# Fused attention and two MLPs on one core: the shared tile of a head pair is moved to second place, and the next pair's Q and K transposes and first scores are moved behind other work

## The chip, the cores and the metric

The kernel runs on one core of a Trainium2 chip. A core has TensorE (PE; its weight loads, which overlap the matmuls, are listed as PEld), VectorE (DVE), ScalarE (ACT), GpSimd (POOL) and SyncE (SP, which here only issues DMAs). The metric is the time of one execution on the device in microseconds (us), as the median of several runs.

## The reference, cut to what matters

```python
B, H, S, D = 4, 8, 576, 64                       # q, k, v: [B, H, S, D]; f: [B, H, S]
scores = (1 / np.sqrt(D)) * np.matmul(q, k.transpose(0, 1, 3, 2))
cum = np.cumsum(np.log(np.clip(f, 0.0001, 1.0)), axis=-1)
decay = cum[:, :, :, None] - cum[:, :, None, :]
scores = np.where(causal, -1e9, scores + decay)  # causal: keys behind the query
attn = softmax(scores)                           # max, exp, sum + 1e-9
x = (attn @ v) laid out as [B * S, H * D]        # 2304 tokens x 512
h = x @ w_in;  x = (h - tanh(h)) @ w_out         # first MLP, 512 -> 2048 -> 512
h = x @ w2_in; out = relu(h) ** 2 @ w2_out       # second MLP, same sizes
```

All of it is float32. The kernel splits operands into a high and a low part of a shorter float format and adds three products, so many matmuls come in twos and threes.

## The kernel before, in words

**Work units.** Attention is cut into 64 units: for each of 32 heads, first the queries 0 to 255 (`hf` 0), then the queries 256 to 575 (`hf` 1, L462). The change concerns the second half, units 32 to 63. Two heads that follow each other make a pair: the even head and the odd head. A unit of the second half has tiles of 128 queries: tile 2 (384 keys), tile 3 (512 keys), and the last 64 queries of *both* heads of a pair share tile 4 (576 keys), which is worked with the even head. Each tile is a **slot** (L465). The slots of a pair are, in order, tiles 2, 3 and 4 of the even head and tiles 2 and 3 of the odd head, named e2, e3, e4, o2 and o3 in this document. A ring of five buffers `Pb` (L369) holds the slots' scores; the one with 640 columns must be that of tile 4 (L466).

**What happens to a slot.** `decay` (L532) writes the decay and the causal mask into the ring's buffer on GpSimd, two slots ahead. It reads a row of `cum` that `load_neg` (L516) has spread over 128 partitions by DMA; there are two such buffers, and the end of `decay` (L559 to L565) loads the row of a later unit. `s_atom` (L732) makes the scores on TensorE from K1 (high part), KLh (low part) and X (Q, both parts); `softmax_of` (L653) takes the maximum on VectorE (L673), the exponential on ScalarE (L682), one over the sum on VectorE and the product with it on GpSimd (L698). Two slots later `pt_atom` (L750) transposes the tile on TensorE (L779); ScalarE copies the high part into PT[0] (L788) and VectorE the low part into PT[1] (L789). For tile 4 a further 128 x 128 block (L774) goes to PT[2] (L793, L795). When the last slot of a head has been transposed, `pv_atoms` (L851) multiplies with the values: atom 0 uses PT[0] in four matmuls (L862) and then PT[2] in one (L866), atom 1 uses PT[1] in four (L862).

**What happens once a pair.** `qk_atoms` (L607) transposes raw k (L629, four matmuls) and raw q (L640, three) of the next pair. ScalarE and VectorE then write K1, KLh and X (L619, L621), and two DMAs copy K1's halves between partitions (L644, L645). There is one K1 and one KLh, so this comes behind the last scores of the pair before.

**What sets the order.** `attn_stream` (L899) yields atoms with a cost (about the columns that TensorE takes). `mlp1_stream` yields atoms of the first MLP (lines L1011 and L1051), 1536 units each in the blocks that lie beside the second half. The loop at L1484 runs the next attention atom when the MLP units done have reached its due time: past the units 0 to 31, 4.65 times the cost of one MLP block (64 x 1536 = 98304 units) is spread evenly over the cost of the 16 pairs. A pair costs 18048 units: scores 5888 (768, 1024 and 2304 for tiles 2, 3 and 4; then 768, 1024), k and q transposes 1792 (1024, 768), values 5504 (even head 1472 and 1216, odd head 1536 and 1280), transposes 4864 (768 for tile 2, 1024 for tile 3, 1280 for tile 4). What follows an atom on other engines is put behind it by a number of steps (`LAG`, L58). From this program order a scheduler makes each engine's list before the run: it goes by priority, and an instruction that it holds not to be ready lets later ones pass. Tiles of PSUM with tag "a" (scores, transposes, values) share four banks.

In the slot loop of `attn_stream` (L908), slot i does in this order: `decay` of slot i + 2; the scores of slot i; at a pair's last slot the k and q transposes of the next pair; the values of a head that has become ready; at an even head's last slot `split_v`, which writes the head pair's values VH; the transposes of slot i - 2.

Of the kernel before, what the change touches and what calls it, by code (L numbers as in the profile page):

```python
# [10 lines left out]
F32 = mybir.dt.float32  # L11
# [7 lines left out]
B, H, S, D = 4, 8, 576, 64  # L19
NT, DM, DFF = B * S, H * D, 2048  # L20
P = 128
# [12 lines left out]
TILES = ([(0, 128, 0, 128), (1, 128, 128, 256)],  # L34
         [(2, 128, 0, 384), (3, 128, 0, 512), (4, 128, 0, 576)])
# [4 lines left out]

PTC = {2: (448, 3), 3: (192, 4)}
XB = (64, 768)
RING = 5
ENDS = (0.5, 1.0, 1.8, 6.45)
UP = (2, 0.1, 1.0)
HOT = 200
# [64 lines left out]
def fused_kernel(ctx: ExitStack, tc: tile.TileContext, q, k, v, f, w1i, w1o, w2i, w2o, out):  # L111
# [8 lines left out]
    ap = actx.enter_context(tc.tile_pool(name="ap", bufs=1))  # L120
# [245 lines left out]
    ident = ap.tile([P, P], F32, name="ident")  # L366
    ccol = ap.tile([P, 5, B * H], F32, name="ccol")
    lfT = ap.tile([P, 5, B * H], F32, name="lfT")
    Pb = [ap.tile([P, 640 if i == RING - 1 else 512], F32, name=f"Pb{i}") for i in range(RING)]  # L369
    mask4 = ap.tile([P, D], F32, name="mask4")  # L370

    st0 = [ap.tile([P, 2, 4], F32, name=f"sp{i}") for i in range(4)]
# [3 lines left out]
    PT, X = [], []  # L376
# [4 lines left out]
    negs = {}  # L381
# [80 lines left out]
    units = [(b, hf, h) for hf in range(2) for b in range(B) for h in range(H)]  # L462
    NU = len(units)
    NH0 = B * H
    slots = [(n, ts) for n in range(NU) for ts in ([TILES[0]] if n < NH0 else [[t] for t in TILES[1][: 3 - n % 2]])]  # L465
    assert all(i % RING == RING - 1 for i, (n, ts) in enumerate(slots) if ts[0][0] == 4)  # L466
    slot0 = {}
    for i, (n, _) in enumerate(slots):
        slot0.setdefault(n, i)
# [42 lines left out]
    def load_done(n):  # L512

        return n >= NH0 or n % 4 == 2

    def load_neg(n):  # L516
        b, hf, h = units[n]
        row = b * H + h
        if hf == 0:
            if n % 2 == 0:  # L520
                t = ap.tile([P, S], F32, tag="neg", name=f"neg_{n}", bufs=2)
                src = cscr[row : row + 1, :256]
                load(t[:, :512].rearrange("p (h k) -> p h k", h=2),
                     bass.AP(tensor=src.tensor, offset=src.offset, ap=[[0, P], [S, 2], [1, 256]]))
                for i in range(2):
                    negs[n + i] = t[:, 256 * i : 256 * i + 256]
        else:
            t = ap.tile([P, S], F32, tag="neg", name=f"neg_{n}", bufs=2)
            nc.sync.dma_start(t, cscr[row : row + 1, :].to_broadcast([P, S]))
            negs[n] = t  # L530

    def decay(i):  # L532
        n, ts = slots[i]
        b, hf, h = units[n]
        if n not in negs:
            load_neg(n)
        t = negs[n]
        pb = Pb[i % RING]
        if len(ts) > 1:
            for ti, rows, o, w in ts:  # L540
                nc.gpsimd.tensor_scalar(pb[:, o : o + w], t[:, :w], ccol[:, ti, b * H + h : b * H + h + 1], 1.0,
                                        op0=ALU.add, op1=ALU.mult)
            x = pb[:, 0:P]
            dg = bass.AP(tensor=x.tensor, offset=x.offset, ap=[x.ap[0], [2 * P, 2], [1, P]])
            nc.gpsimd.affine_select(dg, dg, pattern=[[0, 2], [-1, P]], compare_op=ALU.is_ge, fill=MASK,
                                    base=0, channel_multiplier=1)
        elif ts[0][0] < 4:
            ti, rows, o, w = ts[0]
            nc.gpsimd.tensor_scalar(pb[:rows, o : o + w], t[:rows, :w], ccol[:rows, ti, b * H + h : b * H + h + 1], 1.0,
                                    op0=ALU.add, op1=ALU.mult)  # L550
            dg = pb[:rows, o + ti * P : o + ti * P + rows]
            nc.gpsimd.affine_select(dg, dg, pattern=[[-1, rows]], compare_op=ALU.is_ge, fill=MASK,
                                    base=0, channel_multiplier=1)
        else:
            for x, m in ((slice(0, D), n + 1), (slice(D, P), n)):
                c = b * H + h + m - n
                nc.gpsimd.tensor_scalar(pb[x, :S], negs[m][x, :], ccol[x, 4, c : c + 1], 1.0, op0=ALU.add, op1=ALU.mult)
            nc.gpsimd.tensor_tensor(pb[:, 512:S], in0=pb[:, 512:S], in1=mask4, op=ALU.add)
        nxt = n + 1  # L559
        if n >= NH0:  # L560
            nxt = n + 1 if n % 2 == 0 and ts[0][0] == 2 else n + 2 if ts[0][0] == 4 else NU
        elif slots[i + 1][0] == n:
            nxt = NU
        if nxt < NU and nxt not in negs:
            load_neg(nxt)  # L565

    def split_v(n):
        b, hf, h = units[n]
# [84 lines left out]
    def softmax_of(i):  # L653

        n = slots[i][0]
        b, hf, h = units[n]
        pb = Pb[i % RING]
        hh = h % 2
# [91 lines left out]
    def pt_atom(i):  # L750

        n, ts = slots[i]
        pb = Pb[i % RING]

# [96 lines left out]
    def pv_atoms(n):  # L851
        b, hf, h = units[n]
        hh = h % 2
        nq = NQ[1]
        box = {}

        def a(hl):
            if hl == 0:
                box["t"] = bank("a", 4, f"pv_{n}")
            t = box["t"]  # L860
            for c, (c0, ql, w) in PVC[hh].items():
                nc.tensor.matmul(t[:, ql : ql + w], lhsT=VH[:, hh, c].rearrange("p a d -> p (a d)"),  # L862
                                 rhs=PT[hl][:, c0 : c0 + w], start=hl == 0 and c == 0, stop=hl == 1 and c == 3)
            if hl == 0:
                ql = 256 - 256 * hh
                nc.tensor.matmul(t[:, ql : ql + D], lhsT=VH[:, hh, 4].rearrange("p a d -> p (a d)"),  # L866
                                 rhs=PT[2][:, D - D * hh : 2 * D - D * hh], start=False, stop=False)
            if hl == 1:
                cw.later(LAG['pv'], ev)

        def ev():
            t = box["t"]
            if hh == 0:
                xs_box["t"] = ap.tile([P, 320], F32, tag="xs", name=f"xs_{n}", bufs=2)
            xs = xs_box["t"]
            own = slice(hh * D, hh * D + D)
            oth = slice(D - hh * D, 2 * D - hh * D)
            tmp = ap.tile([P, 320], F32, tag="xtmp", name=f"xt_{n}", bufs=1)
            nc.scalar.activation(tmp[own, :nq], t[oth, :nq], AF.Copy)  # L879

            def fin():
                for c0, d0, w in ((0, 0, nq),) if hh == 0 else ((D, 0, 256), (0, 256, D)):
                    nc.vector.tensor_tensor(xs[own, d0 : d0 + w], t[own, c0 : c0 + w], tmp[own, c0 : c0 + w], op=ALU.add)
                if hh == 1:
                    pair_done(b, hf, h // 2, xs)
            cw.later(LAG['pvadd'], fin)

        cost = sum(max(256, w) for _, _, w in PVC[hh].values())
        return [(cost + 256, lambda: a(0)), (cost, lambda: a(1))]

    def pair_done(b, hf, p, xs):
        if (b, hf) == (0, 0):
# [6 lines left out]
    def attn_stream():  # L899

        yield 0, first_sums, 0
        yield 0, (lambda: (decay(0), decay(1), feed.upload(UP[0]))), 0
        for c, a in kq_atom(0):
            yield c, a, 0

        NS = len(slots)
        pvs, ready = 0, []
        for i in range(NS + 3):  # L908
            if i < NS:
                n, ts = slots[i]  # L910
                last = i + 1 == NS or slots[i + 1][0] != n
                if i == SUMS:
                    yield 0, more_sums, pvs
                if i + 2 < NS:
                    yield 0, (lambda i=i: decay(i + 2)), pvs
                if n % 2 == 0 and n + 2 < NH0:
                    for c, a in kq_atom(n + 2):
                        yield c, a, pvs
                    if load_done(n + 2):
                        yield 0, (lambda: cw.later(LAG['load'], lambda: load_next("qk"))), pvs  # L920
                if n >= NH0:
                    yield *s_atom(i), pvs
                elif n % 2 == 0:
                    yield *s_pair(i), pvs
                if last and n % 2 == 1 and NH0 <= n + 1 < NU:
                    for c, a in qk_atoms(n + 1):
                        yield c, a, pvs
                    yield 0, (lambda: load_next("qk")), pvs
            for m in ready:
                if m >= NH0:  # L930
                    for c, a in pv_atoms(m):
                        yield c, a, pvs
                    pvs += 1
                elif m % 2 == 1:
                    for c, a in pair_atom(m - 1):
                        yield c, a, pvs
                    pvs += 2
            ready = []
            if i < NS and last and n % 2 == 0 and n >= NH0:
                yield 0, (lambda n=n: split_v(n)), pvs  # L940
            if 2 <= i < NS + 2:
                yield *pt_atom(i - 2), pvs
                m = slots[i - 2][0]
                if i - 1 == NS or slots[i - 1][0] != m:
                    ready.append(m)


    xhl = {}
# [585 lines left out]
```

## Time and profile before

| what | us |
|---|---|
| median of three runs | 1048.13 |
| the runs | 1045.79, 1048.13, 1048.20 |
| the profiled execution, its own time | 1042.0 |
| its span, first to last instruction | 1040.3 |
| VectorE busy in the span | 739.5 |
| ScalarE busy | 576.2 |
| GpSimd busy | 425.3 |

The span lies 1.7 us below the time of the execution that was profiled, and that execution lies 3.8 us below the fastest of the three runs. Times in views count from the span's start. In a timeline row the columns are start, duration, engine, line, operation, output and inputs, shape and count; what stands in square brackets is the engine's idle time just before and who ended it. A matmul's end is modelled, so rows of matmuls overlap. A DMA's row on SPq is its issue.

### The profile page before, as it was taken

The numbers are of one execution on the slowest core, as the hardware profiler recorded it, in microseconds if no ns is written. First come the engines' busy times: TensorE is split into PE (matmuls) and PEld (weight loads), VectorE is DVE, ScalarE is ACT, GpSimd is POOL, SyncE is SP. The second block draws the span as 40 slices with busy tenths as digits, with TensorE's granted clock in tenths as the row PEclk, the third lists the DMA queues.
The fourth block names the chain that finished last, engine by engine and source line by source line (L and its number), as shares of the span: only waits on it lengthen the run. The fifth ranks groups of instructions, "written<-read, shape, count | busy, mean of one in ns | idle before, by whom it ended". The sixth has DMA issues, their size and how long they took to land.

```text
span 1040.3 us, 20254 instructions
## 1 busy us (share of the span) xinstructions
PE 1000.9 (96%) x7134; PEld 952.9 (92%) x7134; DVE 739.5 (71%) x1533; ACT 576.2 (55%) x1185; POOL 425.3 (41%) x587
## 2 busy tenths in 40 slices
PE   7989999999999999999999999999999888999998
PEld 5778899999999999999999887999999888999998
DVE  4896963676677766766757578668667969978773
ACT  5885954565666665666645456536455545333331
POOL 3664532354545454555423133395965630000000
PEclk9998999999999999999999999999999989999999
DMA  8946743243343343333203332556777875444431
GB/s 232 275 127 213 213 140 86 72 118 83 78 125 91 90 115 83 107 91 90 78 14 87 102 122 81 169 174 242 226 260 280 274 243 177 142 127 149 132 102 41
DMA packets 184949, 146.97 MB, mean 141 GB/s; under 512 B 86320, under 2 KB 159344, under 8 KB 184848
## 3 DMA queue, kind: packets, MB, share of 16 engines
q1 hardware_dynamic: 184800, 145.65, 46.5%
q8 instruction: 56, 0.92, 0.4%
q14 instruction: 45, 0.37, 0.1%
q10 hardware_dynamic: 48, 0.03, 0.0%
HBM read 101.00 MB, written 39.92 MB: 135 GB/s over the span
## 4 chain that ended last, share of the span: by engine, by line
PE 63%; DVE 8%; POOL 8%; DMA 7%; ACT 6%; issue 6%; SPq 2%; POOLq 0%; ACTq 0%; DVEq 0%
PE o L1371 16%; PE h L1011 14%; PE y L1051 14%; PE pv L862 3%; POOL g L1271 3%; PE r L1221 2%; PE pt L779 2%; PE s L744 2%; PE pv L824 2%; PE s L713 2%; PE s L745 2%; DMA gscr<-g 2%; DMA wscr<-wfull 1%; SPq L151 1%; ACT K L619 1%
## 5 line engine op out<-in xcount | busy, mean ns | idle before, releaser
L1051 PE MATMUL y<-ghl,w 128*128 128x256 f32 (+1 forms) x1536 | 243.1, 302 | 2.8 <-DVE ghl L1032 2.2
L1051 PEld LDWEIGHTS y<-ghl,w 128*128 128x128 f32 x1536 | 210.4, 191 | 16.1 <-DVE ghl L1032 3.5
L1011 PE MATMUL h<-x,w 128*128 128x256 f32 x1344 | 194.9, 289 | 5.5 <-POOL w L228 4.9
L1011 PEld LDWEIGHTS h<-x,w 128*128 128x128 f32 x1344 | 173.5, 191 | 10.5 <-POOL w L228 6.4
L1371 PE MATMUL o<-ws,gc 128*128 128x256 f32 x864 | 117.1, 284 | 0.0
L1347 ACT ACTIVATE gc<-graw 128x1792 fp32r<-128x1792 f32 x35 | 59.4, 1703 | 101.9 <-PE o L1371 59.7
L1221 PE MATMUL r<-yt,ws 128*128 128x384 f32 x576 | 109.1, 337 | 1.6 <-DVE g L1232 1.5
L1371 PEld LDWEIGHTS o<-ws,gc 128*128 128x128 f32 x864 | 110.1, 193 | 0.0
L1271 POOL TENSOR_TENSOR g<-g 128x384 f32<-128x384 f32 (+1 forms) x72 | 84.0, 1185 | 52.6 <-ACT g L1235 47.3
L1221 PEld LDWEIGHTS r<-yt,ws 128*128 128x128 f32 x576 | 101.4, 189 | 2.4 <-DVE g L1232 2.3
L1371 PE MATMUL o<-wq,gc 128*128 128x256 f32 x648 | 92.5, 285 | 5.9 <-ACT gc L1347 5.1
L682 ACT ACTIVATE Pb<-Pb,st 128x384 f32<-128x384 f32 (+2 forms) x80 | 55.2, 690 | 71.1 <-DVE st L673 71.0
L698 POOL TENSOR_SCALAR Pb<-Pb,st 128x384 f32<-128x384 f32 (+2 forms) x80 | 55.2, 690 | 92.0 <-ACT xt L879 45.7
L1371 PEld LDWEIGHTS o<-wq,gc 128*128 128x128 f32 x648 | 84.4, 193 | 6.8 <-ACT gc L1347 5.5
L1221 PE MATMUL r<-yt,wq 128*128 128x384 f32 x432 | 85.0, 341 | 5.1 <-DVE g L1232 3.7
L1221 PEld LDWEIGHTS r<-yt,wq 128*128 128x128 f32 x432 | 77.3, 192 | 6.1 <-DVE g L1232 4.0
L673 DVE CUSTOM_DVE_ANT_0 Pb<-s,Pb 128x128 f32<-128x128 f32 (+4 forms) x144 | 66.8, 479 | 20.2 <-PE s L745 15.0
L1348 DVE TENSOR_TENSOR gc<-graw,gc 128x1792 fp32r<-128x1792 f32 x35 | 71.0, 2032 | 12.9 <-ACT gc L1347 12.8
L1024 DVE TENSOR_TENSOR g<-h,g 128x512 f32<-128x512 f32 x72 | 49.5, 688 | 32.1 <-ACT g L1021 31.5
L1235 ACT ACTIVATE g<-g 128x384 f32<-128x384 f32 x72 | 36.4, 522 | 62.7 <-DVE g L1232 62.4
L1021 ACT ACTIVATE g<-h 128x512 f32<-128x512 f32 x72 | 42.7, 593 | 35.8 <-PE h L1011 30.1
L1032 DVE TENSOR_TENSOR ghl<-g,ghl 128x512 fp32r<-128x512 f32 x72 | 53.7, 746 | 10.6 <-ACT ghl L1028 10.3
(167 smaller groups left out, 1903.5 us busy)
## 6 DMA issues: line engine op xcount, KB each, us to landing
graw<-gscr SPq DMA_DIRECT2D x144, 128.0 KB, 2.4
wraw<-in_moe_w_in_dram SPq DMA_DIRECT2D x32, 512.0 KB, 4.6
wraw<-in_moe_w_out_dram SPq DMA_DIRECT2D x32, 512.0 KB, 5.9
neg<-cscr SPq DMA_DIRECT2D x32, 288.0 KB, 3.3
gscr<-g SPq DMA_DIRECT2D x48, 192.0 KB, 4.0
gscr<-g SPq DMA_DIRECT2D x24, 384.0 KB, 3.5
qk<-in_k_dram SPq DMA_DIRECT2D x48, 128.0 KB, 2.8
v<-in_v_dram SPq DMA_DIRECT2D x48, 128.0 KB, 2.5
```

Of the source, the lines that this page charges most:

```text
L673: nc.vector.tensor_tensor_reduce(out=d, in0=t[:rows, src : src + m], in1=d, scale=-0.125, scalar=3.0e38 if j == 0 else stat(0, x)[:rows], ...
L682: nc.scalar.activation(d, d, AF.Exp, bias=stat(len(parts) - 1, x)[:rows], scale=-1.0, accum_out=stat(2, x)[:rows])
L698: nc.gpsimd.tensor_scalar(d, d, r, 1.0, op0=ALU.mult, op1=ALU.mult)
L1011: nc.tensor.matmul(o, lhsT=win(fc, wh, dc), rhs=xpart(j, dc, xh), start=dc == 0 and wh + xh == 0, stop=dc == ND - 1 and wh == 1)
L1024: nc.vector.tensor_tensor(g, t, g, op=ALU.subtract)
L1032: nc.vector.tensor_tensor(ghl[:, 1], g, ghl[:, 0].bitcast(F32), op=ALU.subtract)
L1051: nc.tensor.matmul(o, lhsT=wout(fc, wh, i * P, P), rhs=ghl[:, xh, fj * n : fj * n + n], start=s == 0 and fj == 0 and wh + xh == 0 and i % ...
L1221: nc.tensor.matmul(t, lhsT=wprod(1, p, k, wh)[:, dc * P : (dc + 1) * P], rhs=yt[i, k][:, xh, dc], start=k in FIRST and dc == 0 and wh + xh ...
L1271: nc.gpsimd.tensor_tensor(g, in0=g, in1=g, op=ALU.mult)
L1347: nc.scalar.activation(hi, t[:, 1:8], AF.Copy)
L1348: nc.vector.tensor_tensor(lo, in0=t[:, 1:8], in1=hi.bitcast(F32), op=ALU.subtract)
L1371: nc.tensor.matmul(o, lhsT=gc[n][gh][:, GWHERE[k], e], rhs=wprod(2, 2 * q + e, k, wh), start=q == 0 and e == 0 and gh + wh == 0 and c0 == ...
```

## The change

The order of a pair's slots becomes e2, e4, e3, o2, o3, and the wide buffer of the ring is the one with index 3. In the slot loop the k and q transposes of the next pair move to the end of slot o3, behind the transposes of slot e3; the scores of e2 move to the end of their slot, behind the even head's values of the pair before and the transposes of o2. PT[2]'s matmul moves from atom 0 of the values to the end of atom 1. The row of `cum` for a head is now loaded by `decay` of tile 3 of the head two places before it, and the first two rows of the second half by the last unit of the first half.

```diff
-RING = 5
+RING, WIDE = 5, 3
...
-    slots = [(n, ts) for n in range(NU) for ts in ([TILES[0]] if n < NH0 else [[t] for t in TILES[1][: 3 - n % 2]])]
-    assert all(i % RING == RING - 1 for i, (n, ts) in enumerate(slots) if ts[0][0] == 4)
+    slots = [(n, ts) for n in range(NU) for ts in ([TILES[0]] if n < NH0 else [[TILES[1][x]] for x in ((0, 2, 1), (0, 1))[n % 2]])]
+    assert all(i % RING == WIDE for i, (n, ts) in enumerate(slots) if ts[0][0] == 4)
...
-        nxt = n + 1
         if n >= NH0:
-            nxt = n + 1 if n % 2 == 0 and ts[0][0] == 2 else n + 2 if ts[0][0] == 4 else NU
-        elif slots[i + 1][0] == n:
-            nxt = NU
-        if nxt < NU and nxt not in negs:
-            load_neg(nxt)
+            nxt = (n + 2,) if ts[0][0] == 3 else ()
+        else:
+            nxt = (n + 1,) if n + 1 < NH0 else (n + 1, n + 2)
+        for m in nxt:
+            if m < NU and m not in negs:
+                load_neg(m)
...
-                                 rhs=PT[hl][:, c0 : c0 + w], start=hl == 0 and c == 0, stop=hl == 1 and c == 3)
-            if hl == 0:
+                                 rhs=PT[hl][:, c0 : c0 + w], start=hl == 0 and c == 0, stop=False)
+            if hl == 1:
                 ql = 256 - 256 * hh
                 nc.tensor.matmul(t[:, ql : ql + D], lhsT=VH[:, hh, 4].rearrange("p a d -> p (a d)"),
-                                 rhs=PT[2][:, D - D * hh : 2 * D - D * hh], start=False, stop=False)
-            if hl == 1:
+                                 rhs=PT[2][:, D - D * hh : 2 * D - D * hh], start=False, stop=True)
                 cw.later(LAG['pv'], ev)
...
-        return [(cost + 256, lambda: a(0)), (cost, lambda: a(1))]
+        return [(cost, lambda: a(0)), (cost + 256, lambda: a(1))]
...
-                if n >= NH0:
+                late = n >= NH0 and n % 2 == 0 and ts[0][0] == 2
+                if n >= NH0 and not late:
                     yield *s_atom(i), pvs
-                elif n % 2 == 0:
+                elif n < NH0 and n % 2 == 0:
                     yield *s_pair(i), pvs
-                if last and n % 2 == 1 and NH0 <= n + 1 < NU:
-                    for c, a in qk_atoms(n + 1):
-                        yield c, a, pvs
-                    yield 0, (lambda: load_next("qk")), pvs
...
+            if i < NS and late:
+                yield *s_atom(i), pvs
+            if i < NS and last and n % 2 == 1 and NH0 <= n + 1 < NU:
+                for c, a in qk_atoms(n + 1):
+                    yield c, a, pvs
+                yield 0, (lambda: load_next("qk")), pvs
```

## Rows read from the trace of the kernel before

**Rows 1.** The page's first part: each engine's busy time, share of the span, instructions.

```profile
PE 1000.9 (96%) x7134; PEld 952.9 (92%) x7134; DVE 739.5 (71%) x1533; ACT 576.2 (55%) x1185; POOL 425.3 (41%) x587
```

**Rows 2.** Stretches: start and end, sum, each engine's busy time, clock, DMA share, GB/s.

```profile
core 0: us, PE busy (x) PEld busy (x) DVE busy (x) ACT busy (x) POOL busy (x), PEclk, DMA share, GB/s
...
170.00:546.00 376.00, 370.62 (x2944) 362.50 (x2943) 255.39 (x705) 226.49 (x533) 179.59 (x304) 1.00 0.34 89
...
830.00:865.00 35.00, 27.68 (x164) 26.87 (x165) 26.70 (x36) 17.91 (x27) 10.19 (x9) 0.85 0.76 249
```

**Rows 3.** Groups of weight loads, 170 to 546 us; last column: idle before, releasers.

```profile
L862 PEld LDWEIGHTS pv<-PT,VH 128*128 128x128 f32 x256 | 38.7, 188 | 3.2 <-DVE PT L789 1.9 <-issue 0.6
...
L744 PEld LDWEIGHTS s<-K,X 128*128 128x128 f32 x128 | 24.2, 189 | 4.7 <-issue 4.2 <-ACT PT L793 0.4
...
L866 PEld LDWEIGHTS pv<-PT,VH 128*128 128x128 f32 x32 | 6.0, 187 | 2.1 <-DVE PT L795 2.1
```

**Rows 4.** Groups of matmuls, 170 to 546 us, the same columns.

```profile
L862 PE MATMUL pv<-PT,VH 128*128 128x320 f32 (+1 forms) x256 | 47.4, 309 | 1.2 <-DVE PT L789 0.9
...
L744 PE MATMUL s<-K,X 128*128 128x288 f32 (+2 forms) x128 | 42.9, 347 | 2.9 <-DMA K<-K 2.1 <-DVE X L621 0.7
...
L866 PE MATMUL pv<-PT,VH 128*128 128x64 f32 x32 | 7.0, 219 | 1.1 <-DVE PT L795 1.1
```

**Rows 5.** Timeline: q's transposes of one pair to its first scores.

```profile
355.67 0.49 PE L640 MATMUL tq<-ident,qk 128*128 128x128 f32 x3
...
356.83 0.60 PE L779 MATMUL pt<-ident,Pb 128*128 128x128 f32 x4
...
357.18 1.67 PE L1011 MATMUL h<-x,w 128*128 128x256 f32 x12
...
358.25 1.58 SPq L645 DMA_DIRECT2D K<-K  x1
...
358.69 1.84 PE L1051 MATMUL y<-ghl,w 128*128 128x256 f32 x14
...
359.03 0.59 ACT L788 ACTIVATE PT<-pt 128x512 fp32r<-128x512 f32 x1
...
359.33 1.06 DVE L621 TENSOR_TENSOR X<-tq,X 64x256 fp32r<-64x256 f32 x3
...
361.11 0.19 PEld L744 LDWEIGHTS s<-K,X 128*128 128x128 f32 x1 [0.79 <-issue]
361.14 0.41 PE L744 MATMUL s<-K,X 128*128 128x384 f32 x1 [0.61 <-DMA K<-K]
...
361.47 0.69 DVE L789 TENSOR_TENSOR PT<-pt,PT 128x512 fp32r<-128x512 f32 x1
```

**Rows 6.** Timeline: o3's transposes, e4's scores and normalisation, the odd head's values.

```profile
365.56 0.60 PE L779 MATMUL pt<-ident,Pb 128*128 128x128 f32 x4
...
365.92 0.96 PE L1011 MATMUL h<-x,w 128*128 128x256 f32 x6
...
366.67 0.58 ACT L788 ACTIVATE PT<-pt 128x512 fp32r<-128x512 f32 x1
366.71 0.29 PE L744 MATMUL s<-K,X 128*128 128x288 f32 x1
...
367.28 0.69 DVE L789 TENSOR_TENSOR PT<-pt,PT 128x512 fp32r<-128x512 f32 x1
...
369.91 0.75 PE L862 MATMUL pv<-PT,VH 128*128 128x320 f32 x4
...
370.53 0.96 PE L1051 MATMUL y<-ghl,w 128*128 128x256 f32 x6
...
370.91 0.76 POOL L698 TENSOR_SCALAR Pb<-Pb,st 128x576 f32<-128x576 f32 x1
```

**Rows 7.** Waits in SP's queue, 170 to 546 us, and landing times of L645.

```profile
SPq L529 <- POOL Pb L552: 46.3, 10, 5.4
...
SPq L644 <- ACT K L619: 9.5, 12, 1.9
...
DMA to landing us min/median/max: 2.4/2.4/3.4
```

More of the change, by code (lines that the diff above doesn't have):

```diff
@@ L368, in fused_kernel @@
     lfT = ap.tile([P, 5, B * H], F32, name="lfT")
-    Pb = [ap.tile([P, 640 if i == RING - 1 else 512], F32, name=f"Pb{i}") for i in range(RING)]
+    Pb = [ap.tile([P, 640 if i == WIDE else 512], F32, name=f"Pb{i}") for i in range(RING)]
     mask4 = ap.tile([P, D], F32, name="mask4")
```

## The prediction, made before the changed kernel was run

> Short names: e2, e3, e4 are the even head's slots of a pair, o2 and o3 the odd head's; e4 holds the tile that both heads share.
>
> **What bounds the kernel now.** I began with the page's first part: TensorE is busy for 96% of the span, every other engine for 71% or less [rows 1], so only what TensorE does or waits for counts. Then the stretches: the change lives where pairs of heads are worked, 170 to 546 us. There matmuls are busy for 370.6 of 376.0 us, weight loads for 362.5, at a granted clock of 1.00, the 2.4 GHz level [rows 2]; VectorE, ScalarE and GpSimd are busy for 255, 226 and 180 us. TensorE is the bound, and a gain can only come from its waits.
>
> Two views give these waits, and they differ. By the groups of weight loads the engine was idle for 4.7 us before the scores L744, 3.2 us before the values L862 and 2.1 us before their fifth part L866 [rows 3]: 10.0 us. By the groups of matmuls it was 2.9, 1.2 and 1.1 us [rows 4]: 5.2 us. Which is right shows at one wait. Fourteen y matmuls start at 358.69 and by the model end at 360.53 [rows 5]. Six MLP matmuls take 0.79 us from first start to the next group's start (365.92 to 366.71), so one is issued every 0.13 us, though each is drawn about 0.29 long [rows 6]. The last y thus began near 360.24 us and its follower could have begun near 360.37. The score began at 361.14: 0.77 us lost, where the weight load's row says 0.79 and the matmul's 0.61 [rows 5]. I take the weight loads' 10.0 us.
>
> The Trainium skill (Perfetto Trace Analysis, Identifying the Most-Contended Engine) says that matmul busy time is a poor measure of what TensorE has left, because matmuls are pipelined, and that the busy share of weight loads is the better one. The trace agrees at this wait (0.77 against 0.79 and 0.61). With the matmuls' groups the sum below would start from 5.2 us in place of 10.0 and end at 2.2, no change.
>
> Why the waits are there: behind the pair's q transposes (355.67 to 356.16) ScalarE, VectorE and a queue's copy must make K and Q; the last copy of K starts at 358.25 and lands about 2.4 us later [rows 5, 7], the last Q part is done at 360.39, and e2's scores start at 361.14, 5.0 us behind the transposes [rows 5]. The transposes of e4 (end 357.43) fall into the same burst: the first half of their result is ready at 359.62, 2.2 us on, the second at 362.16, 4.7 us on [rows 5]. The transposes of o3, outside the burst, have them 1.1 and 1.8 us on (end 366.16; 367.25 and 367.97) [rows 6]. The even head's values need e4's, so they wait.
>
> **The change, part by part.** No matmul, copy or DMA is added or taken away; only places change. Distances come from the planner's costs. Past the first 32 heads it spends 4.65 x 98304 units of MLP on 16 pairs of 18048 units, 1.58 for one. An MLP atom has 1536 units and takes 0.79 us [rows 6], so an attention atom of cost c is followed by c/970 atoms.
>
> *Transposes of q and k earlier against their scores.* Behind the q transposes now come the even head's values, o2's transposes and MLP work: (768 + 2688 + 768)/970 = 4.35 atoms, 3.4 us, and 1.5 us of their own (values 0.62 us, start to start, twice; three transposes 0.27, from four between 365.56 and 365.92 [rows 6]). So e2's scores are due about 5.0 us behind q's transposes, where the pair shown needs 5.0 and waits for 0.79 us, where the mean over 16 pairs is 0.3 [rows 3, 5]. The copies of K are still issued ahead of the next load of raw q and k. What may add to the need: e3's transposes now stand right ahead of k's, so 0.59 us on ScalarE and 0.69 us on VectorE [rows 5] come before or among K's. Bounds for what stays of the 4.7 us: nothing, and all of it. I take 1.4, nearer to nothing, because the room equals the need of a pair with a long wait.
>
> *Even head's values.* They now need e2, e4 and e3; the last is e3, two transposing atoms and 2.9 MLP atoms ahead. Room to the first half: 0.84 + 0.36 + 0.84 + 0.27 + 0.62 (atoms and transposes in turn) less the 0.24 by which a transpose's drawn end lies behind the next start [rows 6] = 2.7 us; to the second, the first half's own 0.55 and 1.0 of MLP more, 4.2 us. The need lies between 1.1 and 1.8 us (a tile outside the burst) and 2.2 and 4.7 us (inside) [rows 5, 6]. The shared tile's own part (L866, 2.1 us of waits [rows 3]) is a slot further back, and its matmul comes last: I cost that wait at nothing. Bounds of what stays for both halves: nothing, and the 3.2 us before L862. I take 1.0, as e3's tile stands at the burst's edge.
>
> *Odd head's values.* Today e4's long scores stand between o3's transposes and these values; now e3's do. Room: 0.84 + 0.47 (1024 columns, by the 1344 that the values take 0.62 us for) + 0.84 less 0.24 = 1.9 us for the first half, 0.55 + 1.04 more, 3.5 us, for the second. The need is 1.1 and 1.8 us by o3's row [rows 6]. Below, nothing (no such wait stands in the list today [rows 3]); above, e4's 4.7 us, 1.2 us a pair, 19 us. I take 0.6 in all, since o3 stays outside the burst.
>
> *e2's scores late, e4's scores straight behind.* From e2's scores to e2's transposes I count 9.6 us (8.2 MLP atoms and 3.1 us of matmuls between), where e4 today goes from first score (366.71) to normalised tile (371.67) in 5.0 us [rows 6]: hidden by 4.6 us. The four shared PSUM banks go round: e4's second bank is the one of the even values, about 3.3 us behind their end, and emptying it takes one ScalarE and one VectorE instruction, no longer than the 0.59 and 0.69 us above [rows 5]. I cost both at nothing; without the cover the price would be about one atom, 0.79 us, a pair.
>
> *Rows of decay loaded two heads ahead.* The number of loads stays. They wait in the DMA queue for GpSimd, 4.6 us on average (46.3 in 10) in most cases [rows 7], and what is queued behind waits too. Today one is issued in o2's slot, one slot before the copies of K; those wait for ScalarE in 12 cases, 0.8 us each [rows 7]. The two loads now belong to e2's slot, behind the copies, and to e3's, two slots ahead of them. A move away from the copies: nothing, with the rival below.
>
> Sum: 10.0 - 1.4 - 1.0 - 0.6 = 7.0 us. The profiled execution took 1042.0 us (span 1040.3), 6.1 below the median of 1048.13; against it the sum gives 1035.0, against the median **1041.1 us**. I carry the whole 7.0 to the end. The place that might change with it is 830 to 865 us, where TensorE is idle for 7.3 of 35 us and the clock is 0.85 on average [rows 2]: 0.3 x 35 = 10.5 us at 1.2 GHz, 5.2 us of work lost. Reached at another moment it may lose a third more or less, an estimate of 1.7 us either way.
>
> **The rivals.** A measurement of this kernel can tell about 0.3% from no change, 3.1 us.
>
> *The waits only change places* (no change). If the burst reaches e3's tile as it does e4's, the even values keep their 3.2 us and the scores half of their 4.7, and the new places add 2 (an estimate, the size of L866's wait): 10.0 - 3.2 - 2.4 - 2.0 = 2.4 us, 1045.7 us. For it: TensorE's order already holds e2's scores back behind 26 MLP matmuls (12 and 14) in the pair shown [rows 5], so the scores may end up as close to K's arrival as now. Against it: the shared tile's wait (2.1 us) has no such twin.
>
> *The odd head's values wait* (slower). Its place is between o3's transposes and L862 for the odd head. If VectorE, which has e4's two maxima ahead of it there, brings the second half as late as e4's today, 4.7 us against 3.5 of room, each pair loses 1.2 us: 19 - 10 = 9 us slower, 1057 us. It decides from 4.1 us on (10.0/16 = 0.62 over the room). Against it: o3's 1.8 us today, 2.3 less than that.
>
> *A load of decay rows stands before the copies of K.* If the order in the queue comes out so, the copies wait for 4.6 us instead of 0.8 [rows 7], and the even pair's scores with them: some 3 us x 16, 48 us, 1087 us. The order of issue speaks against it.
>
> *The change does not do what it says*: TensorE's order is set by priorities and readiness as planned, so the scores may be issued where they were: no change.
>
> **How the numbers follow.** Forecast 0.62; changed places 0.20; no effect 0.06; odd values late 0.09; loads before copies 0.03. So faster 0.62, same 0.26, slower 0.12. The low end takes all 10.0 us and leaves out half of the clock's 1.7, 1037.2; the high end takes in both cases of no change and 0.5 of scatter, 1048.6; the slower ones and a little at either end, less than 0.2, are left out. The forecast's own range is 1037.2 to 1045.0.
>
> **What would show it.** Right: in the groups of weight loads the idle time before L744 falls from 4.7 to near 1.4 us, that before the shared tile's matmul (L866 today) to nothing, and the stretch from 170 us to the end of the pairs is some 6 us shorter. The even head's values wait for about 1 us. Wrong: a wait of the odd head's values for the second half, a wait of the copies of K for GpSimd in the queue's list, or the same stretch with the same idle time at other lines. If the stretch is shorter and the end is not, the carry was wrong, and 830 to 865 us would be longer.

## The result, and the profile after

The changed kernel took 1038.16 us in the median of five runs, against 1048.13 us before. One of the five, the profiled one (1048.58 us, with TensorE at 1.2 GHz from 21 to 59 us, ahead of every changed instruction), is left out of the ratio, 0.9897 with a 95% interval from 0.9853 to 0.9941, which compares the means of the other runs. Measured again in run e1 below, the ratio was 0.9903 (0.9873 to 0.9932), 10.2 us faster. The change is about 1%, and both intervals lie wholly below 1: faster, as forecast. The forecast was 7.0 us faster, and 1038.16 lies inside the range of 1037.2 to 1048.6. The profile shown here is that of e1 (its own time 1041.87 us). The engines' busy times are those of before [rows 1] within 3 us:

```profile
PE 1000.1 (96%) x7134; PEld 955.3 (92%) x7134; DVE 739.1 (71%) x1533; ACT 576.2 (55%) x1185; POOL 428.2 (41%) x587
```

The stretch of the pairs, in the view of [rows 2]. Weight loads are busy for 370.5 of 376.0 us where they were for 362.5:

```profile
170.00:546.00 376.00, 374.17 (x3019) 370.47 (x3018) 260.12 (x712) 230.93 (x540) 182.67 (x304) 1.00 0.35 92
```

The groups of weight loads in that stretch, as in [rows 3]; the last column is the idle time before them:

```profile
L1013 PEld LDWEIGHTS h<-x,w 128*128 128x128 f32 x1008 | 131.5, 190 | 3.0 <-DVE x L967 1.7
...
L862 PEld LDWEIGHTS pv<-PT,VH 128*128 128x128 f32 x256 | 38.3, 188 | 0.1
L744 PEld LDWEIGHTS s<-K,X 128*128 128x128 f32 x128 | 24.2, 189 | 0.9 <-issue 0.5 <-ACT PT L788 0.2
...
L866 PEld LDWEIGHTS pv<-PT,VH 128*128 128x128 f32 x32 | 6.0, 188 | 0.0
```

The idle time before the scores fell from 4.7 to 0.9 us and that before the values from 5.3 to 0.1: 9.0 of 10.0 us are gone. One new wait stands against it, of 1.7 us, once, at an MLP matmul for a block's input; with it the idle time of that group (L1011 before, in the row below) rose from 1.9 to 3.0 us. 9.0 - 1.1 = 7.9 us.

```profile
L1011 PEld LDWEIGHTS h<-x,w 128*128 128x128 f32 x984 | 126.9, 190 | 1.9 <-DVE x L965 0.4 <-ACT x L964 0.3
```

That the stretch became shorter by just this shows in k's transposes, one group of four a pair. Their rows, of before and then of after; the last two times are the start of the first and of the last matmul:

```profile
L629 PE MATMUL tk<-ident,qk x64: 270/272/273, 170.9 to 511.9; 128*128 128x128 f32 x64
```

```profile
L629 PE MATMUL tk<-ident,qk x64: 272/272/273, 175.4 to 508.5; 128*128 128x128 f32 x64
```

341.0 us became 333.1. From the first group's start to the last group's start it is 340.6 and 332.7, and this figure, called the distance below, is used for all runs: 7.9 us less. It is a sharp measure: two profiles of the kernel before have 340.64 and 340.63, two of the change 332.86 and 332.70.

One pair after the change, from e3's transposes to the next e2's scores, the counterpart of [rows 5]:

```profile
334.09 0.60 PE L779 MATMUL pt<-ident,Pb 128*128 128x128 f32 x4
...
335.24 0.58 ACT L788 ACTIVATE PT<-pt 128x512 fp32r<-128x512 f32 x1
...
335.85 0.69 DVE L789 TENSOR_TENSOR PT<-pt,PT 128x512 fp32r<-128x512 f32 x1
335.85 0.34 SPq L529 DMA_DIRECT2D neg<-cscr  x1
335.88 1.21 ACT L619 ACTIVATE K<-tk 64x512 fp32r<-64x512 f32 x2
...
336.39 0.49 PE L640 MATMUL tq<-ident,qk 128*128 128x128 f32 x3
...
337.43 0.69 PE L862 MATMUL pv<-PT,VH 128*128 128x320 f32 x4
...
337.99 0.55 SPq L645 DMA_DIRECT2D K<-K  x1
...
338.70 0.69 PE L862 MATMUL pv<-PT,VH 128*128 128x320 f32 x4
...
339.03 1.06 DVE L621 TENSOR_TENSOR X<-tq,X 64x256 fp32r<-64x256 f32 x3
...
341.25 0.41 PE L744 MATMUL s<-K,X 128*128 128x384 f32 x1
```

Both halves of e3's tile are ready at 335.82 and 336.54, 1.1 and 1.9 us behind its transposes: on ScalarE and on VectorE the tile's copy comes ahead of K's and Q's. The values that need them start at 337.43 and 338.70. The last Q part is done at 340.09, 3.2 us behind q's transposes (4.2 in the pair of [rows 5]); the scores start 4.4 us behind them.

### The profile page after: what moved, and what is told of

Its sections match the earlier page's. It is cut to its first block, busy times and chain, and to the rows that moved or that the text cites. A ratio compares the mean times of both kernels' runs of the same rounds, so it can differ in the third digit from the quotient of the medians.

```text
span 1046.9 us, 20277 instructions
## 1 busy us (share of the span) xinstructions
PE 1012.2 (97%) x7134; PEld 964.5 (92%) x7134; DVE 739.5 (71%) x1533; ACT 576.1 (55%) x1185; POOL 426.7 (41%) x587
## 5 line engine op out<-in xcount | busy, mean ns | idle before, releaser
L1013 PE MATMUL h<-x,w 128*128 128x256 f32 x1344 | 198.7, 289 | 6.3 <-POOL w L228 4.3
L1013 PEld LDWEIGHTS h<-x,w 128*128 128x128 f32 x1344 | 175.6, 191 | 11.1 <-POOL w L228 5.8
L682 ACT ACTIVATE Pb<-Pb,st 128x384 f32<-128x384 f32 (+2 forms) x80 | 55.3, 691 | 67.0 <-DVE st L673 66.6
```

The lines of the kernel that those rows point to most:

```text
L682: nc.scalar.activation(d, d, AF.Exp, bias=stat(len(parts) - 1, x)[:rows], scale=-1.0, accum_out=stat(2, x)[:rows])
L1013: nc.tensor.matmul(o, lhsT=win(fc, wh, dc), rhs=xpart(j, dc, xh), start=dc == 0 and wh + xh == 0, stop=dc == ND - 1 and wh == 1)
```

## The experiments

The theory to test was the prediction's: ScalarE's, VectorE's and the queue's work behind k's and q's transposes is a burst, and what counts is which tile stands inside it and how far behind it the first scores are. Its first rival was that the shared tile's place, as the last tile ahead of the even head's values, is the cause.

**e1, the whole change again.** No edit.

> The whole change once more, for a second profile of it. Theory of the burst (the copies that follow k's and q's transposes on ScalarE and VectorE are late; what counts is how far behind them the first scores and the even head's values stand): in the weight loads' groups of the stretch of the pairs the idle time before L744 is about 1 us (4.7 before), before L862 and L866 together under 1 us (5.3 before); from the first to the last k transposes about 333 us (340.6 before); ratio 0.988 to 0.993. Rival theory, a different start of the execution (the clock's early stretches) made the first result: those idle times are the same but the ratio lies within 0.3% of 1.

Measured: ratio 0.9903 (0.9873 to 0.9932), distance 332.7 us, idle 0.9 us before L744 and 0.1 before L862 and L866. The start's clock is no cause of the gain: in the first 100 us the granted clock was 0.91 on average in e1's profile and 0.95 in that of before.

**e2, the two moves alone.**

```diff
+                late = n >= NH0 and n % 2 == 0 and ts[0][0] == 2
-                if n >= NH0:
+                if n >= NH0 and not late:
                     yield *s_atom(i), pvs
...
-                if last and n % 2 == 1 and NH0 <= n + 1 < NU:
-                    for c, a in qk_atoms(n + 1):
-                        yield c, a, pvs
-                    yield 0, (lambda: load_next("qk")), pvs
...
+            if i < NS and late:
+                yield *s_atom(i), pvs
+            if i < NS and last and n % 2 == 1 and NH0 <= n + 1 < NU:
+                for c, a in qk_atoms(n + 1):
+                    yield c, a, pvs
+                yield 0, (lambda: load_next("qk")), pvs
```

> Only the two moves (k's and q's transposes behind the slot's weight transposes, e2's scores behind the even head's values); the slots keep the order e2, e3, e4, o2, o3, and PT[2] stays in the first values atom. Theory of the burst: e4's transposes now stand ahead of the burst, so the values' waits go nearly as well: idle before L744 under 1.5 us, before L862 and L866 together under 2 us, ratio 0.989 to 0.993, as the whole change. Theory of the shared tile (its place as the last tile before the even head's values is the cause of their waits): L744 under 1.5 us, but L862 and L866 keep 4 to 5 us, ratio 0.994 to 0.997.

Measured: ratio 0.993 (0.9902 to 0.9958), distance 334.5 us. The groups of weight loads:

```profile
L862 PEld LDWEIGHTS pv<-PT,VH 128*128 128x128 f32 x256 | 38.5, 188 | 0.1
L744 PEld LDWEIGHTS s<-K,X 128*128 128x128 f32 x128 | 24.3, 189 | 3.6 <-ACT PT L788 1.5 <-issue 1.0 <-ACT ghl L1031 0.8
L866 PEld LDWEIGHTS pv<-PT,VH 128*128 128x128 f32 x32 | 6.0, 188 | 0.0
```

The values' waits are gone with the shared tile still in its old place: the rival falls. But 3.6 us stay before the scores, where the theory expected under 1.5: a miss that e9 to e12 follow up. The moves bring 6.2 of the 7.9 us of distance.

**e3, the order of the slots alone**: the change's edits outside `attn_stream`, without its two moves.

> Only the order of the slots e2, e4, e3, o2, o3 with its ring, its loads of rows and PT[2]'s matmul last; the transposes of q and k and e2's scores stay where they were. Theory of the burst: e3's transposes fall into the burst in e4's place: L744 keeps 4 to 5 us, L862 keeps 2 to 4 us, only L866's 2.1 us goes; ratio 0.996 to 1.000. Theory of the shared tile: L862 and L866 go to under 1 us together, L744 keeps 4 to 5 us, ratio 0.993 to 0.996.

Measured: ratio 0.9977 (0.9955 to 1.0), distance 340.5 us.

```profile
L862 PEld LDWEIGHTS pv<-PT,VH 128*128 128x128 f32 x252 | 38.1, 188 | 4.1 <-DVE PT L789 3.4 <-ACT PT L788 0.5
L744 PEld LDWEIGHTS s<-K,X 128*128 128x128 f32 x128 | 24.2, 189 | 4.6 <-issue 2.3 <-ACT g L1020 1.5 <-ACT ys L1060 0.4
L866 PEld LDWEIGHTS pv<-PT,VH 128*128 128x128 f32 x31 | 5.8, 188 | 0.0
```

As the burst has it: e3's tile takes e4's place in the burst, the values wait for 4.1 us before L862 (3.2 before), the scores keep 4.6, and only L866's wait goes.

**e4, late scores alone**: of e2's edit the lines with `late`; k's and q's transposes stay in their old place.

> Only e2's scores move behind the even head's values and o2's transposes; k's and q's transposes stay right behind o3's scores, and the slots keep their order. Theory of the burst: e2's scores have some 6.6 us of room, L744 goes to under 0.5 us; but e4's transposes are still inside the burst (need 2.2 and 4.7 us) and the values now come without e2's scores between, so L862 and L866 together rise from 5.3 to 8 us or more; ratio 0.996 to 1.01. Theory of the shared tile predicts 5.3 us as before there, so a ratio near 0.9955.

Measured: ratio 1.0075 (1.0047 to 1.0104), distance 346.5 us, slower. The groups, and three rows of one pair's timeline:

```profile
L862 PEld LDWEIGHTS pv<-PT,VH 128*128 128x128 f32 x242 | 36.0, 188 | 17.0 <-ACT PT L788 14.8 <-DVE PT L789 1.4
L744 PEld LDWEIGHTS s<-K,X 128*128 128x128 f32 x128 | 24.2, 189 | 0.0
```

```profile
342.02 0.93 ACT L619 ACTIVATE X<-tq 64x256 fp32r<-64x256 f32 x3
...
343.15 0.59 ACT L788 ACTIVATE PT<-pt 128x512 fp32r<-128x512 f32 x1
...
343.79 0.59 PEld L862 LDWEIGHTS pv<-PT,VH 128*128 128x128 f32 x4 [1.01 <-ACT PT L788]
```

With room the scores wait for nothing. The values, which e2's scores no longer hold back, now wait for the copy of e4's tile that ScalarE makes behind Q's three. The 4.7 us before the scores went, and 11.7 came before the values.

**e5, the kernel before, profiled once more.** No edit.

> The kernel before, unchanged, for a second profile of it. Both theories: from the first to the last k transposes 340 to 341.5 us, idle before L744, L862 and L866 together 9 to 11 us, as in the first profile; if these differ by more than 1 us, the differences between the other profiles are not to be read to the microsecond.

Measured: distance 340.6 us, idle 3.9 + 3.8 + 2.5 = 10.2 us. The sum repeats; how it is split between scores and values moves by 0.8 us.

**e6, the transposes alone**: of e2's edit all but the lines with `late`.

> Only k's and q's transposes move, behind the transposes of e4; the slots keep their order and e2's scores stay at the head of their slot. Theory of the burst: e4's transposes now stand ahead of the burst, so L862 and L866 together fall from 5.3 to under 1.5 us, but between q's transposes and e2's scores only about one MLP atom is left, so the idle time before L744 rises from 4.7 to 8 us or more; ratio 0.997 to 1.004. Theory that the scores' place alone counts (late scores are what helps): the values' waits stay at 4 us or more.

Measured: ratio 1.001 (0.9983 to 1.0036), distance 343.7 us.

```profile
L862 PEld LDWEIGHTS pv<-PT,VH 128*128 128x128 f32 x251 | 38.4, 189 | 0.0
L744 PEld LDWEIGHTS s<-K,X 128*128 128x128 f32 x128 | 24.2, 189 | 12.8 <-issue 8.8 <-ACT ghl L1028 3.6 <-DVE xs L883 0.4
...
L866 PEld LDWEIGHTS pv<-PT,VH 128*128 128x128 f32 x31 | 5.8, 188 | 0.0
```

The mirror of e4: the values are free of the burst, the scores wait for 12.8 us. Either move alone lengthens the distance, by 5.9 us (e4) and 3.0 us (e6); together they shorten it by 6.2.

**e7, PT[2]'s matmul last alone.** As in the change's `pv_atoms`.

> Only the matmul of PT[2] moves from the first to the second values atom; everything else as before. Theory of the burst: L866's 2.1 us go, but the second half of PT, which VectorE makes right behind PT[2]'s, is as late as before, so L862 takes over a part: L862 and L866 together 3 to 5 us (5.3 before), L744 as before; ratio 0.997 to 1.000. Rival (the shared tile's own part is a wait of its own, behind nothing): together 3.2 us and no more, ratio 0.998. A result under 2 us would speak against the burst.

Measured: ratio 1.0003 (0.9977 to 1.0029), distance 340.2 us.

```profile
L862 PEld LDWEIGHTS pv<-PT,VH 128*128 128x128 f32 x256 | 38.5, 188 | 5.9 <-DVE PT L789 4.3 <-issue 0.6
L744 PEld LDWEIGHTS s<-K,X 128*128 128x128 f32 x128 | 24.3, 190 | 3.7 <-issue 3.2 <-ACT PT L793 0.4
L866 PEld LDWEIGHTS pv<-PT,VH 128*128 128x128 f32 x32 | 6.0, 188 | 0.0
```

L866's wait went and L862's took it over: 5.9 us together, where I expected 3 to 5. VectorE makes PT[2]'s part and then the second half of PT; waiting for the one had hidden the wait for the other.

**e8, less room**: the whole change, with e2's scores ahead of o2's transposes.

```diff
             ready = []
+            if i < NS and late:
+                yield *s_atom(i), pvs
...
-            if i < NS and late:
-                yield *s_atom(i), pvs
```

> The whole change, but e2's scores stand right behind the even head's values, ahead of o2's transposes: about 0.9 us less room behind q's transposes. Theory of the burst: the need (3.6 us in the middle, 4.1 at most in the whole change) is now about the room, so the idle time before L744 rises from 0.9 to 2 to 6 us; L862 and L866 stay under 0.5 us; ratio 0.991 to 0.996. Rival (any place behind the values will do, the scheduler fills in): L744 stays at 1 us, ratio 0.990.

Measured: ratio 0.9981 (0.9955 to 1.0007), distance 339.6 us.

```profile
L744 PEld LDWEIGHTS s<-K,X 128*128 128x128 f32 x128 | 24.2, 189 | 8.3 <-ACT VH L572 4.4 <-issue 2.5 <-ACT xs L845 0.9
```

The right direction, and more than expected (8.3 against 2 to 6 us): 6.9 of the 7.9 us of distance are lost. One MLP atom and three transposes of room went: without their own wait the scores start 3.2 us behind q's transposes in most pairs, 4.2 in e1. Over 16 pairs some 17 us of room were taken away and 7.4 us of waits came, so not every microsecond was needed; Q's last part is done 3.6 us behind the transposes in the middle and 4.1 at most, in both.

**e9, e10, e11, the loads of decay rows.** Why do the two moves alone keep 3.6 us before the scores? In e2 the copies of K (L644) land 3.0 us behind their issue in the middle and 5.1 at most, in e1 2.4 and 4.0. A row load of 288 KB is issued ahead of them in both; in the kernel before it goes out behind them. e9 is e2 with another place for the load of the even row, e10 the whole change with the same, e11 is e2 with the odd row's load a slot earlier; the edits replace the condition in `decay`:

```diff
-            nxt = n + 1 if n % 2 == 0 and ts[0][0] == 2 else n + 2 if ts[0][0] == 4 else NU
+            nxt = n + 1 if ts[0][0] == 2 else NU                                              # e9, on e2
-            nxt = (n + 2,) if ts[0][0] == 3 else ()
+            nxt = (n + 2,) if n % 2 and ts[0][0] == 3 else (n + 1,) if n % 2 else ()          # e10, on the change
-            nxt = n + 1 if n % 2 == 0 and ts[0][0] == 2 else n + 2 if ts[0][0] == 4 else NU
+            nxt = (n + 2,) if ts[0][0] == (3 if n % 2 else 4) else ()                         # e11, on e2
```

> The two moves alone, with the old order of slots, as in e2_places_only, but the row of decay for the next even head is loaded by o2's decay in place of e4's, so behind the copies of K and not 1.7 us ahead of them. Theory of the row load (in e2_places_only the copies of K land 3.0 us after issue and not 2.4, because the 288 KB row load moves in front of them): the copies land in 2.3 to 2.4 us in the middle, the idle time before L744 falls from 3.6 to about 1 us, ratio 0.989 to 0.992. Rival theory (the shared tile's two evacuations ahead of k's are what keeps L744 at 3.6): landing falls, but L744 keeps 3 us or more, ratio 0.993.

> The whole change with the same later row load: the next even head's row by o2's decay in place of e3's. Theory of the row load: nearly nothing is left to gain, since the copies already land in 2.4 us in the middle; only the few late ones (up to 4.0 us) go: idle before L744 from 0.9 to under 0.6 us, ratio 0.988 to 0.992. Rival (the load is now too late for its own decay): POOL waits for the row and L673 for POOL, and the ratio is above 0.993.

> A control to e9: the two moves alone with the old order of slots, where the odd head's row is loaded a slot earlier (by o3's decay) and the even head's row stays where it is in e2_places_only. Theory of the row load: it is the even head's row that stands ahead of the copies, so nothing changes: landing 2.9 to 3.1 us in the middle, idle before L744 3 to 4.5 us, ratio 0.991 to 0.996. Rival (any row load moved away helps): L744 under 2 us.

Measured: e9 0.9922 (0.9897 to 0.9946), distance 334.5, L744 3.7 us; e10 0.9903 (0.9874 to 0.9931), 332.8, 1.1 us; e11 0.991 (0.9881 to 0.9938), 333.5, 2.7 us. The copies land in 2.9, 2.4 and 3.0 us in the middle. e9 did not do what it was meant to: the queue of one of its pairs, where the row load L529 still stands 1.1 us ahead of the copies, as in the same pair of e2 (293.81 and 294.95):

```profile
293.13 0.32 SPq L529 DMA_DIRECT2D neg<-cscr  x1
293.80 0.38 SPq L488 DMA_DIRECT2D qk<-in_k_dram  x1
294.27 0.51 SPq L644 DMA_DIRECT2D K<-K  x1
```

In e1, e2 and e9 alike this load goes out 0.03 us behind the GpSimd instruction that reads its buffer last: the scheduler issues it as soon as the buffer is free, though e9 has it a slot later in the program. In e10 too it stands where it stood in e1, about 2.2 us ahead of the copies in the middle. So e9 and e10 say nothing of the theory; e11, meant as a control, lost 0.9 us of L744 that I had not expected it to lose, and no run shows why.

**e12, row loads of 4 KB in place of 288**, on e2: the transfer's bytes are taken away, and the four computing engines' instructions keep their order. Left out is the decay along a row: one column serves all keys.

```diff
-            nc.sync.dma_start(t, cscr[row : row + 1, :].to_broadcast([P, S]))
+            nc.sync.dma_start(t[:, :8], cscr[row : row + 1, :8].to_broadcast([P, 8]))
...
-            nc.gpsimd.tensor_scalar(pb[:rows, o : o + w], t[:rows, :w], ccol[:rows, ti, b * H + h : b * H + h + 1], 1.0,
+            nc.gpsimd.tensor_scalar(pb[:rows, o : o + w], t[:rows, :1].to_broadcast([rows, w]), ccol[:rows, ti, b * H + h : b * H + h + 1], 1.0,
...
-                nc.gpsimd.tensor_scalar(pb[x, :S], negs[m][x, :], ccol[x, 4, c : c + 1], 1.0, op0=ALU.add, op1=ALU.mult)
+                nc.gpsimd.tensor_scalar(pb[x, :S], negs[m][x, :1].to_broadcast([D, S]), ccol[x, 4, c : c + 1], 1.0, op0=ALU.add, op1=ALU.mult)
```

> The two moves alone with the old order of slots, as in e2_places_only, but each row of decay of the second half is loaded as 8 columns in place of 576 (4 KB in place of 288), and decay uses its first column for all keys; so the decay inside a row is left out, and the order of the four computing engines is the same instruction by instruction. Theory of the row load (its bytes in flight delay the copies of K that follow it by 1.1 to 2.4 us): the copies land in 2.3 to 2.5 us in the middle in place of 2.9 to 3.0, the idle time before L744 falls from 3.6 to under 1.5 us, first to last k transposes 333 us or less (334.5). Rival theory (the two evacuations of the shared tile ahead of k's): the landing may fall, but L744 keeps 3 us or more and the distance stays at 334.5.

Measured: ratio 0.9899 (0.987 to 0.9928), distance 331.2 us. The times from issue to landing of L644 in e2 and in e12, and the scores' group in e12:

```profile
DMA to landing us min/median/max: 2.3/3.0/5.1
```

```profile
DMA to landing us min/median/max: 2.3/2.4/2.9
```

```profile
L744 PEld LDWEIGHTS s<-K,X 128*128 128x128 f32 x128 | 24.2, 189 | 0.7 <-issue 0.7
```

Without the bytes the copies land in 2.4 us, the scores' wait falls from 3.6 to 0.7 us, and the distance by 3.3. The evacuations of the shared tile were still there, so that rival falls: the row load is what e2 has left. The pairs of e2 show the same one by one: where the row load went out 1.1 to 1.5 us ahead of the copy (five pairs), the copy landed in 3.6 to 5.1 us; where it went out 2.2 to 2.4 us ahead, in 2.3 us in four pairs and 3.5 in one. The load of raw k (L488, 128 KB) is nearer to the copy in the first five as well, by some 0.5 us; only e12, which leaves that load as it is, parts the two. e12's distance is 1.5 us below even the whole change's; the weight loads of the MLP's first layer are idle for 1.5 us in it as in e2, for 2.5 in e3 and for 3.0 in e1, so the MLP's new wait comes with the new slot order.

The Trainium skill (DMA: Bandwidth & Descriptors, Queues, rings and completion order) says that a DMA's completion lands only after every earlier write of the same DMA engine. The traces agree with it (2.4 against 3.0 us in the middle, 2.9 against 5.1 at most), though they can't tell this order from a share of bandwidth.

## Why the prediction was right

*The budget.* Ten microseconds of waits by the weight loads' rows, not 5.2 by the matmuls', was the right reading. 9.0 us of idle time went, 1.1 came, and the distance fell by 7.9 us. By the matmuls' groups (5.2 us to 0.4, and 0.1 to 1.4 at the MLP; the rows of e1 stand below) it should have fallen by 3.5. The Trainium skill's rule on weight loads (Perfetto Trace Analysis, Identifying the Most-Contended Engine) thus holds here over the whole stretch.

```profile
L1013 PE MATMUL h<-x,w 128*128 128x256 f32 x1009 | 148.6, 287 | 1.4 <-DVE x L967 1.4
...
L862 PE MATMUL pv<-PT,VH 128*128 128x320 f32 (+1 forms) x256 | 46.2, 302 | 0.0
...
L744 PE MATMUL s<-K,X 128*128 128x288 f32 (+2 forms) x128 | 42.6, 344 | 0.4 <-DMA K<-K 0.3
```

*What stays.* The sum took off 3.0 us for waits that stay; 1.0 stayed, and this is the step that was mis-sized. It had no term for the new wait at the MLP, 1.1 us; that the total came within 0.9 us of the distance is thus partly luck. For the scores 1.4 was taken and 0.9 measured. The room was shorter than worked out (4.2 us in most pairs, and 4.4 with its wait in the pair shown, not 5.0), but the need shrank as well: Q's last part is done 4.0 us behind its transposes in the middle of the 16 pairs before and 3.6 us after. One reason stands in the timeline of before: ScalarE works the exponential of o3's scores (L682) among K's copies, in the pair of [rows 5] and in four others, and in no pair of e1.

```profile
355.16 0.60 ACT L619 ACTIVATE K<-tk 64x512 fp32r<-64x512 f32 x1 [0.83 <-PE tk L629]
...
355.95 0.72 ACT L682 ACTIVATE Pb<-Pb,st 128x512 f32<-128x512 f32 x1 [0.20 <-DVE st L673]
...
356.79 0.59 ACT L619 ACTIVATE K<-tk 64x512 fp32r<-64x512 f32 x1
```

I had taken the need of the kernel before for granted and only added to it. For the even values 1.0 was taken and 0.1 measured. The room was right (2.7 and 4.0 us, worked out as 2.7 and 4.2), but e3's tile is not "at the burst's edge": in the pair shown its copies come ahead of K's on both engines, and it needs 1.1 and 1.9 us. For the odd values 0.6 was taken and no wait is listed; that rival, at 0.09, had no trace of itself.

*The parts.* The prediction costed the two moves, the slots and the row loads one by one, which hid that the moves only work together (e4 slower, e6 the same, e2 faster). The wait of L866 that it costed "at nothing" is no gain of its own either (e7).

*The row loads.* The step "a move away from the copies" was wrong. The row load of the next even head stands ahead of the copies in the queue, 1.5 us in the pair shown, the least of 15 pairs, and about 2.2 in the middle, because the scheduler issues it as soon as GpSimd has freed its buffer. It did not hold the copies in the queue, as the rival had it; its bytes delay their landing. (The rival's price is also off by a little: 48 us on the forecast's 1041.1 are 1089, not 1087.) In the new slot order the last decay that reads this buffer is e3's, in the old one e4's, which GpSimd works in two halves of some 0.75 us; so the load starts earlier against the copies (2.2 us ahead, not 1.7), and they land in 2.4 us, not 3.0. That this, and not the shared tile's own wait, is what the slot order adds on top of the moves (1.8 us of distance) is argued from issue times, the pairs of e2 and e12; no run moved the load alone.

*The carry.* 7.9 us are shown in the distance, which leaves out the last pair. From the last scores of the first half (L713) to the first product of the second MLP the profiles of before have 497.0 and 499.2 us (the second with 3.4 us at 1.2 GHz in it) and those of the change 488.0 and 487.7: at least 9.0 us less. The whole execution gained 10.2 us, with an interval from 7.1 to 13.3, so the gain was carried, and no more than scatter is left to explain. Behind that point, in code that the change leaves alone, both kernels scatter alike: to the last matmul 378.3 and 382.6 us before, 383.7 and 378.4 after. This is also why the profiled execution of e1 (1041.9 us) is no shorter than that of before (1042.0): it spent 3.5 us more ahead of the pairs and 5.4 us more in the second MLP.

No version beat the change by more than the intervals tell: e10 has the same ratio, e11 0.991. A version with the two moves, the old slots and the row loads held behind the copies was not made.

## What to carry to other kernels

When a burst of work on in-order engines makes results for two readers, here the values and the first scores, moving only one of them moved the wait to the other (e4, e6). Move the start of the burst behind what the first reader needs, and the second reader behind other work, in the same change, and compare the room with the need of each. Price a wait of TensorE by the weight loads' idle time, and check it by the distance between two equal instructions some pairs apart, which repeated here to 0.01 us (before) and 0.2 us (the change) while whole executions differed by over 5 us. Look at what is already in flight on the DMA engines when a short copy on the critical path is issued.

## What I had not expected of the hardware

A copy of 144 KB inside SBUF landed 2.4 us behind its issue in the middle and 2.9 at most in e12; with a 288 KB load issued some 1.7 us ahead of it, as in e2, it took 3.0 us in the middle and up to 5.1, although that load is no dependence of it. And the half-speed stretch of the clock before 60 us, which differed from profile to profile, did not touch the distance between the pairs: 332.9 us in the profile that had 37 us at 1.2 GHz and 332.7 in e1.
